# Attention with mixed heads: scores as scaled float16 parts on row halves, premix on array quarters, float32 postmix with the sums folded in

## The chip, the cores and the metric
The kernel runs on one core of a Trainium2 chip. The metric is device time in microseconds, the median of several executions. TensorE (PE) multiplies matrices and writes PSUM, VectorE (DVE), ScalarE (ACT) and GpSimd (POOL) work elementwise, and SyncE (SP) issues the transfers. An array quarter is one half of TensorE's rows with one half of its columns.

## The reference
Two batches, 12 heads, 448 tokens, head size 64; model width 768. The scores of all heads are mixed by a 12 x 12 matrix before the softmax, and the softmax's results by another after it. Then follow an RMS norm, a gated block (768 to 1536 to 768) and a second block (768 to 2048 to 768).

```python
scores = scale * np.matmul(q, k.transpose(0, 1, 3, 2))
scores = np.einsum('bhij,hg->bgij', scores, w_pre)
attn = np.exp(scores - np.max(scores, axis=-1, keepdims=True))
attn = attn / (np.sum(attn, axis=-1, keepdims=True) + 1e-09)
attn = np.einsum('bhij,hg->bgij', attn, w_post)
x = np.matmul(attn, v)                       # to [tokens, 768]
xn = x / np.sqrt(np.mean(x * x, -1) + 1e-6) * rms_g
x = (silu(xn @ w_gate) * (xn @ w_val)) @ w_out
out = elu(x @ w_in2) @ w_out2
```

## The kernel before
Operands are split in a high and a low part, x = h + l, and three products (hh, hl, lh) are summed in PSUM.

The attention has a first stage and a loop. In the first stage the q and k of the first batch are turned by TensorE to [head size, token] (`k_turn`, `q_turn`) and split. q's two parts stand one above the other on 128 partitions, and k twice, so that `scores` (L407, L408) needs two 128-row products per head and chunk of 112 query rows. ScalarE copies the scores out of PSUM as float32 (`scores_out`, L418), and a transfer puts them into the DRAM tensor `s_d`, as [query row, head, key].

The loop takes 90 groups, 45 for each batch. A group is ten query rows with all heads, 120 partitions (row, head), read back from `s_d` two groups at a time into `sg` (`load_group`). Its steps are, each for another group at the same time:
- premix (`g_premix`): a 120 x 120 matrix with `w_pre` on its diagonal blocks. Every other group takes float32 as it is (L476), the others split parts (`g_split` on ScalarE, L468, and GpSimd, L469; products L479 to L481).
- the maximum on VectorE (L488), the exponential with its sum on ScalarE (L496), the sum's reciprocal (L504, L511).
- the exponentials over their sum, as float16 parts `eh` (L524 on ScalarE or L526 on VectorE) and `el` (L533 on VectorE).
- postmix (`g_postmix`, L554): four chunks of 112 keys, three float16 products each, which also turn the result.
- `g_out` (L566): ScalarE copies the result into `at`, and after six or seven groups a window's product with v follows (L590), the norm, and the split of the normed tokens.

Between these steps a list `hq` is worked off at fixed rates per step (`FAST`, `RATE`, `LATE`): the first batch's other score chunks, then the turning of the second batch, then its scores. All engines take their instructions in the program's order. Five PSUM tiles (`psa`) serve scores, premix and turning alike. `psa` tiles are given out as they are freed in the program's order.

After the attention, weights come as float64, are converted to split parts beside the products (`convert`), with the norm's weights `g_sb` multiplied into gate and value weights, and TensorE goes through all products of the two blocks.

## Time and profile before
| | us |
|---|---|
| median of 3 runs | 789.88 (789.84 to 791.38) |
| span of the profiled execution | 787.3 |
| TensorE busy | 759.4 |
| VectorE busy | 550.6 |
| ScalarE busy | 445.6 |
| GpSimd busy | 114.4 |

The profiled execution's own time is its span, from the first to the last instruction; the runs' times include what lies around it. Busy time counts records, and the records of matmuls reach to their modelled end, so two that follow each other overlap: the price of a matmul is read from one start to the next. PEld is the loading of weights, which runs beside matmuls.

### The profile page before, as it was taken

To read this page: it belongs to the slowest core of one execution; us is meant where nothing else is said; L and a number is where in the kernel's file an instruction comes from. 1 tells how busy PE (TensorE), PEld (TensorE's weight loads), DVE (VectorE), ACT (ScalarE), POOL (GpSimd) and SP (SyncE) were. 2 spreads that over 40 slices of the span, in tenths; PEclk is the share of its full clock that TensorE was granted. 3 is DMA by queue.
4 is the path that set the end of the run, shared out by engine and by line. 5 is a ranking of instruction groups with operands and counts; after the bars stand their busy time and mean duration, and the time that the engine had idled before them with its cause. 6 is when DMAs were issued, how large, how long until landed. Compare 5 with 4: busy or idle time off the path is not lost.

```text
span 787.3 us, 14708 instructions
## 1 busy us (share of the span) xinstructions
PE 759.4 (96%) x5655; PEld 673.1 (85%) x5655; DVE 550.6 (70%) x1135; ACT 445.6 (57%) x952; POOL 114.4 (15%) x141
## 2 busy tenths in 40 slices
PE   6779999999998999999999999999999999999997
PEld 5557778777776779999999999999999999999997
DVE  6356999665789938887877865652898887553651
ACT  7679888887987925654544433231576566221320
POOL 4212565333443400000000000000000000000000
PEclk9899999999998999999999999999999999999999
DMA  7798665668783303343332333231444343433512
GB/s 205 222 280 252 168 154 140 178 173 236 217 230 78 104 2 121 122 132 108 121 112 94 116 121 106 95 121 41 121 132 120 109 122 100 111 111 111 155 47 70
DMA packets 90249, 105.42 MB, mean 134 GB/s; under 512 B 16004, under 2 KB 86084, under 8 KB 90180
## 3 DMA queue, kind: packets, MB, share of 16 engines
q1 hardware_dynamic: 90180, 104.49, 46.0%
q8 instruction: 44, 0.72, 0.4%
q14 instruction: 25, 0.20, 0.1%
HBM read 82.46 MB, written 22.02 MB: 133 GB/s over the span
## 4 chain that ended last, share of the span: by engine, by line
PE 83%; DVE 7%; DMA 5%; ACT 2%; issue 1%; SPq 1%; POOL 1%; ACTq 0%; POOLq 0%
PE psa_t L197 13%; PE psa_t L198 13%; PE psa_t L199 13%; PE psv_t L590 5%; PE pst_t L554 4%; PE psf_t L198 4%; PE psf_t L199 4%; PE psf_t L197 4%; PE psa_t L966 3%; PE psa_t L964 3%; PE psa_t L965 3%; DMA s_d<-st 3%; PE psa_t L476 3%; DMA sg<-s_d 2%; PE psa_t L407 2%; DVE el L533 1%
## 5 line engine op out<-in xcount | busy, mean ns | idle before, releaser
L554 PEld LDWEIGHTS <-eh 120*112 120x112 f16 x720 | 66.8, 131 | 27.2 <-issue 21.8
L240 ACT ACTIVATE whl<-w 128x768 fp32r<-128x768 f32 x44 | 37.1, 844 | 86.0 <-PE psf_t L966 28.5
L244 ACT ACTIVATE whl<-w,g_sb 128x128 fp32r<-128x128 f32 x144 | 45.0, 393 | 64.1 <-PE psa_t L199 25.6
L219 ACT ACTIVATE w<-raw 128x768 f32<-128x768 f32 x68 | 62.5, 919 | 30.5 <-DVE whl L251 23.6
L469 POOL TENSOR_TENSOR sl<-sg,sh 120x448 fp32r<-120x448 f32 (+1 forms) x45 | 54.5, 1211 | 116.2 <-ACT sh L468 111.6
L251 DVE TENSOR_TENSOR whl<-w,whl 128x768 fp32r<-128x768 f32 x44 | 42.2, 958 | 41.1 <-ACT whl L240 40.0
L198 PE MATMUL psa_t<-x2l,whl 128*128 128x448 f32 x192 | 70.1, 365 | 0.0
L199 PE MATMUL psa_t<-x2h,whl 128*128 128x448 f32 x192 | 70.1, 365 | 0.0
L197 PE MATMUL psa_t<-x2h,whl 128*128 128x448 f32 x192 | 70.1, 365 | 0.0
L233 DVE SCALAR_TENSOR_TENSOR w<-w,raw 128x768 int32<-128x768 int32 x68 | 65.2, 958 | 2.3
L554 PE MATMUL pst_t<-m2h,eh 120*112 120x120 f16 x360 | 63.0, 217 | 2.7 <-ACT at L566 2.6
L227 DVE SCALAR_TENSOR_TENSOR raw<-raw 128x768 int32<-128x768 int32 x68 | 64.8, 953 | 0.0
L554 PE MATMUL pst_t<-m2h,el 120*112 120x120 f16 x360 | 63.1, 218 | 1.7 <-DVE el L533 1.7
L496 ACT ACTIVATE e<-psa_t,nmax 120x448 f32<-120x448 f32 (+1 forms) x90 | 58.0, 645 | 11.4 <-DVE rs L511 10.4
L533 DVE SCALAR_TENSOR_TENSOR el<-e,rs,eh 120x448 f16<-120x448 f32 (+1 forms) x90 | 64.0, 711 | 0.3 <-ACT eh L524 0.3
L554 PE MATMUL pst_t<-m2l,eh 120*112 120x120 f16 x360 | 63.0, 218 | 0.0
L488 DVE TENSOR_REDUCE nmax<-psa_t 120x1 f32<-120x448 f32 (+1 forms) x90 | 55.2, 613 | 8.4 <-PE psa_t L481 8.3
L197 PE MATMUL psa_t<-xh,whl 128*128 128x448 f32 x150 | 55.7, 372 | 1.0 <-ACT xh L640 1.0
L590 PE MATMUL psv_t<-at,vs 112*64 112x70 f32 (+3 forms) x1344 | 55.7, 230 | 0.0
L590 PEld LDWEIGHTS psv_t<-at,vs 112*64 112x64 f32 x1344 | 46.5, 139 | 9.9 <-issue 7.0
L198 PE MATMUL psa_t<-xl,whl 128*128 128x448 f32 x150 | 54.9, 366 | 0.0
L199 PE MATMUL psa_t<-xh,whl 128*128 128x448 f32 x150 | 54.8, 365 | 0.0
(167 smaller groups left out, 2059.2 us busy)
## 6 DMA issues: line engine op xcount, KB each, us to landing
raw<-in_moe_w_out_dram SPq DMA_DIRECT2D x28, 768.0 KB, 4.5
sg<-s_d SPq DMA_DIRECT2D x44, 420.0 KB, 5.0
s_d<-st SPq DMA_DIRECT2D x93, 196.0 KB, 3.2
raw<-in_moe_w_in_dram SPq DMA_DIRECT2D x16, 768.0 KB, 4.7
raw<-in_moe_w_gate_dram SPq DMA_DIRECT2D x12, 768.0 KB, 4.3
raw<-in_moe_w_val_dram SPq DMA_DIRECT2D x12, 768.0 KB, 4.4
vs<-in_v_dram SPq DMA_DIRECT2D x4, 672.0 KB, 7.7
kt<-in_k_dram SPq DMA_DIRECT2D x12, 224.0 KB, 3.8
```

The costliest lines, as they stand in the source:

```text
L197: nc.tensor.matmul(out=ps, lhsT=wh(kk), rhs=xh_(kk), start=(first and kk == 0), stop=False)
L198: nc.tensor.matmul(out=ps, lhsT=wh(kk), rhs=xl_(kk), start=False, stop=False)
L199: nc.tensor.matmul(out=ps, lhsT=wl(kk), rhs=xh_(kk), start=False, stop=(last and kk == nk - 1))
L219: nc.scalar.activation(out=w, in_=raw.bitcast(F32)[:, :, 1], func=ACTF.Copy, scale=REBASE)
L227: nc.vector.scalar_tensor_tensor(out=lo, in0=hi, scalar=SIGN, in1=lo, op0=ALU.bitwise_and, op1=ALU.bitwise_or)
L233: nc.vector.scalar_tensor_tensor(out=wi, in0=wi, scalar=3, in1=lo, op0=ALU.logical_shift_left, op1=ALU.bitwise_or)
L469: nc.gpsimd.tensor_tensor(out=sl[:r], in0=s32, in1=sh[:r].bitcast(F32), op=ALU.subtract)
L488: nc.vector.tensor_reduce(out=nmax[:r], in_=ps[:r, :S], axis=AXX, op=ALU.max, negate=True)
L496: nc.scalar.activation(out=e32[:r], in_=ps[:r, :S], func=ACTF.Exp, bias=nmax[:r], scale=1.0, accum_out=sm[:r])
L533: nc.vector.scalar_tensor_tensor(out=el[:r], in0=e32[:r], scalar=rs[:r], in1=eh[:r], op0=ALU.mult, op1=ALU.subtract)
L554: nc.tensor.matmul(out=o, lhsT=lhs[:r, c * CP:(c + 1) * CP], rhs=rhs[:r, :, :ni], start=(n == 0), stop=(n == 2),)
L590: nc.tensor.matmul(out=psx[s * D:(s + 1) * D, kk, :n], lhsT=vs[b][:, hh, c, :], rhs=at[:, c, hh, :n], start=(c == 0), stop=(c == NCH - 1),)
```

## The change
- **Scores.** q and k of two heads are turned side by side, so that one head stands on partitions 0 to 63 and the other on 64 to 127 (`turn`). `scores` makes three products per head, each on its half of TensorE's rows, alternating between the two heads and writing a PSUM tile for each. The result is multiplied by a scale per head, `alpha`, from the largest q and k, and leaves as two float16 parts: the high one by ScalarE, the low one by VectorE. `s_d` holds both, in the same bytes.
- **Premix.** A group's ten rows are two halves of five rows (60 partitions at 0 and 64). Two groups are premixed together in float16, three products for each half, on the four quarters of the array. The split of `sg`, the whole-float32 form and their knobs are gone. The scale is taken back in the exponential (`esc`).
- **Postmix.** The exponentials stay float32. The reciprocal sums are multiplied into the postmix matrix by GpSimd (`g_scale`), and the postmix is one float32 product per chunk. `eh` and `el` are gone, and the loop has one step of lag less. Of the copies out of the postmix every other one goes to VectorE.
- **Norm weights.** They are multiplied into the tokens by GpSimd in the window's chain, no longer into the gate and value weights.
- The rates and the head start of `hq` are set anew; the first row chunk's scores come after all heads are turned, since `alpha` needs the largest values of all.

```diff
-            nc.tensor.matmul(out=ps[:CP, :S], lhsT=lhs, rhs=kh, start=True, stop=False)
-            nc.tensor.matmul(out=ps[:CP, :S], lhsT=lhs, rhs=kl, start=False, stop=True)
+            for n, (i, j) in enumerate(((0, 0), (0, 1), (1, 0))):
+                for s in range(2):
+                    d = slice(s * D, (s + 1) * D)
+                    nc.tensor.matmul(
+                        out=pss[s][:CP, :S], lhsT=qkt[d, 0, i, c * CP:(c + 1) * CP], rhs=qkt[d, 1, j],
+                        start=(n == 0), stop=(n == 2),
+                    )
+            def high(s):
+                a = alpha[b][:CP, 2 * p + s:2 * p + s + 1]
+                nc.scalar.activation(out=st[:, s, 0], in_=pss[s][:CP, :S], func=ACTF.Copy, scale=a)
+            def low(s):
+                a = alpha[b][:CP, 2 * p + s:2 * p + s + 1]
+                nc.vector.scalar_tensor_tensor(
+                    out=st[:, s, 1], in0=pss[s][:CP, :S], scalar=a, in1=st[:, s, 0], op0=ALU.mult, op1=ALU.subtract
...
-            nc.scalar.activation(out=sh[:r], in_=s32, func=ACTF.Copy)
-            nc.gpsimd.tensor_tensor(out=sl[:r], in0=s32, in1=sh[:r].bitcast(F32), op=ALU.subtract)
...
-                nc.tensor.matmul(out=ps[:r, :S], lhsT=m1f[:r, :r], rhs=sg.pop((b, g))[:r], start=True, stop=True)
-                nc.tensor.matmul(out=ps[:r, :S], lhsT=m1h[:r, :r], rhs=sh[:r], start=True, stop=False)
-                nc.tensor.matmul(out=ps[:r, :S], lhsT=m1l[:r, :r], rhs=sh[:r], start=False, stop=False)
-                nc.tensor.matmul(out=ps[:r, :S], lhsT=m1h[:r, :r], rhs=sl[:r], start=False, stop=True)
+            pss = [ps_a() for _ in range(n)]
+            for i, (m, x) in enumerate(((m1h[b], 0), (m1l[b], 0), (m1h[b], 1))):
+                for j in range(n):
+                    for s in range(2):
+                        c = s ^ j
+                        a = slice(s * Q, s * Q + min(HB, (rows_of(g + j) - c * HI) * H))
+                        nc.tensor.matmul(
+                            out=pss[j][c * Q:(c + 1) * Q, :S], lhsT=m[a], rhs=t[a, j, x],
+                            start=(i == 0), stop=(i == 2),
+                        )
...
-                nc.vector.tensor_scalar_mul(eh[:r], e32[:r], rs[:r])
-            nc.vector.scalar_tensor_tensor(
-                out=el[:r], in0=e32[:r], scalar=rs[:r], in1=eh[:r], op0=ALU.mult, op1=ALU.subtract
-            )
+            nc.gpsimd.tensor_scalar_mul(m2s[:GQ], m2f[:GQ], rs[:GQ])
...
-                for n, (lhs, rhs) in enumerate(((eh, m2h), (eh, m2l), (el, m2h))):
-                    nc.tensor.matmul(
-                        out=o, lhsT=lhs[:r, c * CP:(c + 1) * CP], rhs=rhs[:r, :, :ni],
-                        start=(n == 0), stop=(n == 2),
-                    )
+                nc.tensor.matmul(
+                    out=o, lhsT=e32[:GQ, c * CP:(c + 1) * CP], rhs=m2s[:GQ, :, :ni], start=True, stop=True
+                )
...
-        EARLY, FAST, RATE, LATE = 4, 1.5, 1.4, 1.4
+        EARLY, FAST, RATE, LATE = 2, 0.75, 1.1, 0.6
```

On TensorE, in the loop's first third, before: a head's scores, the premix of a group in split parts, and the beginning of its postmix (`eh`, `el` are the exponentials' parts, `m2h` and `m2l` the postmix matrix's).

```order
L407 MATMUL psa_t<-par 112x448
L408 MATMUL psa_t<-par 112x448
L479 MATMUL psa_t<-sh,m1h 120x448
L480 MATMUL psa_t<-sh,m1l 120x448
L481 MATMUL psa_t<-sl,m1h 120x448
L554 LDWEIGHTS eh
L554 MATMUL pst_t<-m2h,eh 112x120
L554 LDWEIGHTS eh
L554 MATMUL pst_t<-m2l,eh 112x120
L554 LDWEIGHTS el
L554 MATMUL pst_t<-m2h,el 112x120
```

On TensorE at the same place now, with buffer numbers and the semaphores that are waited for: the last two of a premix's twelve quarter products, the postmix, and the scores of two heads.

```order
L478 LDWEIGHTS m1h0_108
L478 MATMUL psa_t_890<-sg_717,m1h0_108 64x448
L533 MATMUL pst_t_909<-m2s_857,e32_820 112x120 [waits PE_49,Activation_49,Pool_49]
L533 MATMUL pst_t_909<-m2s_857,e32_820 112x120 x3
L408 MATMUL psa_t_915<-par_190 112x448 [waits DVE_49]
L408 MATMUL psa_t_916<-par_190 112x448 [waits Activation_49]
L408 MATMUL psa_t_915<-par_190 112x448
```

The postmix now waits for GpSimd's scaled matrix, the first score tile for VectorE's low part of an earlier score, and the second for ScalarE.

On VectorE, two steps while the second batch is scored, before: sum, maximum, reciprocal, low part, and in one of them the high part.

```order
L504 TENSOR_SCALAR sm<-sm 120x1
L488 TENSOR_REDUCE nmax<-psa_t 120x1
L511 RECIPROCAL rs<-sm 120x1
L533 SCALAR_TENSOR_TENSOR el<-e_2428,rs,eh 120x448
L504 TENSOR_SCALAR sm<-sm 120x1
L488 TENSOR_REDUCE nmax<-psa_t 120x1
L511 RECIPROCAL rs<-sm 120x1
L533 SCALAR_TENSOR_TENSOR el<-e_2483,rs,eh 120x448
L526 TENSOR_SCALAR eh<-e_2554,rs 120x448
```

On VectorE two such steps now, of which one has scores of two heads and a copy out of the postmix.

```order
L505 TENSOR_SCALAR sm<-sm 124x1
L488 TENSOR_REDUCE nmax<-psa_t 124x1
L489 TENSOR_SCALAR nmax<-nmax,esc_106 124x1
L509 RECIPROCAL rs<-sm 124x1
L419 SCALAR_TENSOR_TENSOR st<-psa_t,alpha_105,st 112x448 x2
L616 TENSOR_TENSOR xt<-xt,psa_t 128x420
L505 TENSOR_SCALAR sm<-sm 124x1
L488 TENSOR_REDUCE nmax<-psa_t 124x1
L489 TENSOR_SCALAR nmax<-nmax,esc_106 124x1
L509 RECIPROCAL rs<-sm 124x1
L419 SCALAR_TENSOR_TENSOR st<-psa_t,alpha_105,st 112x448 x2
L548 COPY at<-pst_t 112x48x10
```

The parts of the exponentials are gone from VectorE; low parts of the scores, a scaling of the maximum and copies of the postmix stand there instead, behind the maximum of the same step.

## Rows read from the trace of the kernel before
**Rows 1.** Stretches, the loop and the products after it: busy us of each engine (instructions).
```profile
core 0 of [0], span 787.3 us
core 0: us, PE busy (x) PEld busy (x) DVE busy (x) ACT busy (x) POOL busy (x), PEclk, DMA share, GB/s
39.40:273.10 233.70, 222.27 (x2700) 173.44 (x2699) 183.90 (x493) 197.48 (x476) 97.24 (x112) 0.99 0.69 186
293.60:700.00 406.40, 406.35 (x2032) 378.79 (x2033) 302.93 (x524) 197.21 (x383) 0.00 (x0) 1.00 0.36 111
```
**Rows 2.** Timeline of TensorE in the loop: start, duration, engine, line, operation, tiles.
```profile
134.72 1.01 PE L476 MATMUL psa_t<-sg,m1f 120*120 120x448 f32 x2
135.57 0.22 PE L554 MATMUL pst_t<-m2h,eh 120*112 120x120 f16 x1
...
136.18 0.44 PE L407 MATMUL psa_t<-par 128*112 128x448 f32 x1
136.46 0.37 PE L408 MATMUL psa_t<-par 128*112 128x448 f32 x1
136.66 0.34 PE L631 MATMUL psa_t<-dg,ones 70*128 70x70 f32 x2
136.80 0.44 PE L479 MATMUL psa_t<-sh,m1h 120*120 120x448 f32 x1
137.08 0.37 PE L480 MATMUL psa_t<-sh,m1l 120*120 120x448 f32 x1
137.28 0.36 PE L481 MATMUL psa_t<-sl,m1h 120*120 120x448 f32 x1
137.49 0.21 PE L554 MATMUL pst_t<-m2h,eh 120*112 120x120 f16 x1
...
139.06 1.15 PE L590 MATMUL psv_t<-at,vs 112*64 112x60 f32 x32
140.14 1.01 PE L476 MATMUL psa_t<-sg,m1f 120*120 120x448 f32 x2
```
**Rows 3.** Timeline earlier in the loop: turning k and q; weight loads of a premix.
```profile
102.42 0.56 PE L379 MATMUL psa_t<-ident,kt 112*128 112x112 f32 x4
...
102.75 0.51 PE L393 MATMUL psa_t<-identr,qn 112*128 112x112 f32 x4
...
107.94 0.28 PEld L476 LDWEIGHTS psa_t<-sg,m1f 120*120 120x120 f32 x2
```
**Rows 4.** VectorE by line in the loop: count, busy us, mean ns, idle before.
```profile
L533 DVE SCALAR_TENSOR_TENSOR el<-e,rs,eh 120x448 f16<-120x448 f32 (+1 forms) x88 | 62.6, 712 | 0.0
L488 DVE TENSOR_REDUCE nmax<-psa_t 120x1 f32<-120x448 f32 (+1 forms) x89 | 54.5, 613 | 0.1
L526 DVE TENSOR_SCALAR eh<-e,rs 120x448 f16<-120x448 f32 (+1 forms) x40 | 24.9, 623 | 0.0
...
L504 DVE TENSOR_SCALAR sm<-sm 120x1 f32<-120x1 f32 (+1 forms) x89 | 13.2, 149 | 53.3 <-ACT e L496 52.6
...
L386 DVE TENSOR_TENSOR par<-psa_t,par 128x448 fp32r<-128x448 f32 x7 | 4.3, 611 | 0.0
```
**Rows 5.** ScalarE by line in the loop.
```profile
L496 ACT ACTIVATE e<-psa_t,nmax 120x448 f32<-120x448 f32 (+1 forms) x89 | 57.4, 645 | 11.4 <-DVE rs L511 10.4 <-DVE nmax L488 0.9
L566 ACT ACTIVATE at<-pst_t 112x480 f32<-112x480 f32 (+1 forms) x86 | 50.5, 587 | 1.0 <-PE pst_t L554 0.9
...
L524 ACT ACTIVATE eh<-e,rs 120x448 f16<-120x448 f32 x48 | 32.7, 681 | 0.0
L468 ACT ACTIVATE sh<-sg 120x448 fp32r<-120x448 f32 (+1 forms) x43 | 25.2, 585 | 6.0 <-DMA sg<-s_d 4.9 <-POOL sq L605 0.9
L496 ACT ACTIVATION_READ_ACCUMULATOR e<-psa_t,nmax 120x1 f32 (+1 forms) x89 | 19.3, 217 | 0.0
```
**Rows 6.** GpSimd by line in the loop.
```profile
L469 POOL TENSOR_TENSOR sl<-sg,sh 120x448 fp32r<-120x448 f32 (+1 forms) x44 | 53.3, 1212 | 107.5 <-ACT sh L468 102.9 <-PE psa_t L481 4.3
...
L604 POOL TENSOR_TENSOR sq<-sq 128x210 f32<-128x210 f32 (+2 forms) x11 | 8.7, 795 | 0.9
```
**Rows 7.** Timeline, the first softmax exponential.
```profile
39.39 0.63 ACT L496 ACTIVATE e<-psa_t,nmax 120x448 f32<-120x448 f32 x1
```

More of the change, by code (lines that the diff above doesn't have):

```diff
@@ L47, in block_kernel @@
     GP = GI * H
+    HI = GI // 2
+    HB = HI * H
+    Q = P // 2
+    GQ = Q + HB
     NG = -(-S // GI)
@@ new lines, in post @@
+        def post():
+            ps = ps_a()
+            nc.tensor.matmul(
+                out=ps[:, :H], lhsT=selr.rearrange("p s r -> p (s r)"), rhs=wpo, start=True, stop=True
+            )
+            for s in range(2):
+                h = slice(s * Q, (s + 1) * Q)
+                nc.vector.tensor_tensor(
+                    out=m2f[h, :, s * HI:(s + 1) * HI], in0=mask[h].rearrange("p i g -> p g i"),
+                    in1=ps[h, :H].unsqueeze(2).to_broadcast([Q, H, HI]), op=ALU.mult,
+                )
@@ L707, in attention @@
         fast = len(hq)
-        hq += [lambda: q_split(*heads[H])]
-        hq += [f for i in range(H, 2 * H) for f in turn(i)]
+        for p in range(NP):
+            hq.append(lambda p=p: turn(1, p, 0))
+            hq.append(lambda p=p: (turn(1, p, 1), p + 2 < NP and load_qk(1, p + 2)))
+        hq += scales(1)
         turned = len(hq)
-        hq += [f for c in range(NCH) for f in rows(1, c)]
+        hq += [lambda p=p, c=c: scores(1, p, c) for c in range(NCH) for p in range(NP)]
         seq = [(b, g) for b in range(B) for g in range(NG)]
@@ L747, in fill @@
                 gates.pop(0)()
-        for t in range(-6, n + 5):
+        for t in range(-6, n + 4):
             if LG * 2 <= t + 5 < n and seq[t + 5][1] % LG == 0:
```

532 lines of the change are left out of this document (238 added, 294 removed).

## The prediction
> **What bounds it now.** I read the table of stretches first, for where TensorE has room, then its timeline in the loop for the price of each form, then the other engines' groups by line. The profiled execution spans 787.3 us [rows 1], which lies 2.6 us under the median of 789.88, which I keep as the constant around the span. From 293.6 us on, TensorE is busy 406.35 of 406.40 us up to 700 [rows 1]: the weight products are bound by TensorE and nothing of the change touches their matmuls. The merged scaling of the gate and value weights (one instruction for six on ScalarE and on VectorE) is worth nothing there; it would matter only if conversion became late, and VectorE is idle a quarter of that stretch. So the question is the attention part: 39.4 us until the first softmax, a loop of 90 groups (ten rows each) in 233.7 us, a tail of 20.5 us.
>
> In the loop TensorE is busy 222.3 us of 233.7 and so waits 11.4 us in all; ScalarE is busy 197.5 and VectorE 183.9 [rows 1]. A group takes 2.60 us: TensorE sets it, and the other two are close behind. The timeline of TensorE [rows 2] gives its prices, start to start, since matmuls overlap in their records:
> - a 448-column pass of split float32: 0.20 us (137.08 to 137.28);
> - the same after another form of instruction: 0.28 (136.18 to 136.46, 136.80 to 137.08), so a change of form costs some 0.08 to 0.10;
> - the whole-float32 premix: 0.85 (134.72 to 135.57), about 0.75 of it for 448 columns in two records, 0.10 the change;
> - the split premix: 0.69 (136.80 to 137.49);
> - a postmix of twelve float16 products of 120 columns: 0.61 (135.57 to 136.18);
> - a head's score chunk: 0.48 (136.18 to 136.66), 0.40 when another stands before it; I use 0.45;
> - the v product of one window piece, 32 records of 60 columns on two column halves: 1.08 (139.06 to 140.14). At the premix's price per column (0.75 us for 896) one after another they would take 1.6, so column halves do overlap.
>
> **The change, part by part, on TensorE.**
> Premix. Two groups cost 0.85 + 0.69 = 1.54; 45 such pairs are 69. After it, 12 products of 448 columns serve two groups, four to a pass, one in each quarter of the array. If quarters overlap: 3 x 0.20 + 0.10 = 0.70, 45 pairs 32, **-38**. If only column halves do: 1.30 a pair, -11. If nothing does: 2.50, +43. I take the first: the v product shows column halves overlapping; row halves no row shows.
> Scores. 84 heads' chunks (96 less the 12 ahead of the loop) cost 84 x 0.45 = 38. After it a pair of heads takes three passes on two row halves: 0.70 if they overlap, so 42 x 0.70 = 29, **-9**; one after the other 1.30, +17.
> Postmix. Twelve float16 products become four float32 ones of two records. By the premix's column price, 120 x 0.75/448 = 0.20 each, 0.80 for four, 0.90 with the change of form, against 0.61: 90 x 0.29 = **+26**. Without the change of form +17. The far bound is weight loads that nothing hides: 0.28 for two [rows 3], 1.12 for eight, +101. The v product is the nearer row, float32 records with few columns and a weight load each: 1,920 columns in 1.08, so 960 in 0.54, and with no halves to overlap 0.80, the matmul price itself. I keep +26.
> Turning the second batch. A head's two turns cost 0.33 for k (102.42 to 102.75 [rows 3]) and about as much for q; 12 heads 8. After it twelve turns of a pair, 4: **-4**.
> TensorE in all: -38 - 9 + 26 - 4 = **-25**, from 222 to 197 us of 90 groups, 2.19 a group.
>
> **The other engines.** VectorE loses the second parts (62.6) and first parts (24.9) of the exponentials [rows 4] and twelve casts of q (0.61 each, 7). It gains a second part for each score chunk, 84 between the 0.611 of L386 (same PSUM source) and the 0.712 of L533 (same operation); at 0.64, 54. It also gains half the copies out of the postmix, 45 of 480 columns at L386's rate, 29; 90 more single-column operations at 0.149, 13; and twelve maxima, 5. Sum +101 - 95 = +6: 190 us. ScalarE loses L468 (25.2), L524 (32.7), half of L566 (25) and the q splits: from 197 to about 110 [rows 5]. GpSimd loses 53.3 us of L469 and the q splits, and gains 90 scalings of 120 columns (0.80 for 210 columns [rows 6]; by the column 0.45, in all 41) and fourteen multiplications by the norm's weights (by the column 1.6 at most, 22). It stays near 110 us, off the path; but the scaling stands between the sum of a row and the postmix, two steps later, so a late one is waited for by TensorE directly. The transfers move the same bytes, two float16 values for a float32, the stores in half as many issues; at a share of 0.69 in the loop [rows 1] they stay hidden at 2.4 us a group too. A store now waits in SP's queue for VectorE's second part instead of ScalarE's copy, and the loads of later groups stand behind it; they are issued five steps ahead of their premix, which covers a step's delay.
>
> So TensorE stays the longest engine with 197, VectorE comes to 190, and ScalarE has room. The gain of 25 is not all kept. While the second batch is turned, a step's VectorE work is 0.61 maximum, three times 0.15, 0.33 copy, 1.1 x (0.61 + 0.40) for the turns and 0.27 for the windows, 2.77; reduced like its sum for overlapping ends by a seventh (the loop's 21 groups by line, the largest in [rows 4], sum to 218, its busy time is 183.9) 2.35, against 2.15 on TensorE: 23 steps x 0.2 = 5. And the PSUM tiles: five in all; a premix now takes two at once, the second held a step longer, and a score tile is freed by VectorE's second part, which stands behind the maximum, where before ScalarE freed it first thing in the step. TensorE's waits in the loop were 11.4; I add half again, 6. Together **+11**.
>
> Start and tail. The first batch's scores now wait until all six pairs are turned and the largest q and k are known; before, head 0 was scored while head 2 was turned. ScalarE's 24 copies and the 12 second parts (12 x 0.61 = 7.3) fill that time, while the old first step was held up anyway until 39.39 [rows 7]. I take **+2**, between 0 and +8. The loop's lag is one step shorter; the last windows have one more multiplication on GpSimd: **-1**.
>
> Sum: 787.3 - 25 + 11 + 2 - 1 = 774.3; with the 2.6 around the span, **777 us**.
>
> **A rule against it.** The row that bears on the quarters is the v product: two halves that write different partitions of one PSUM tile overlap, 1.08 against 1.6 [rows 2]. It has two column halves and one set of rows. The Trainium skill, TensorEngine Tiling (Array Packing), section Restrictions and Gotchas, says that different row tiles cannot access the same PSUM bank at the same time. The trace cannot contradict it. By it, the first two quarters of a pass, which are on different rows and write one tile, would follow one another. The same page (Tiling Modes, Key Properties) says that a change of mode drains the engine; the trace agrees with a cost, 0.08 to 0.10 us a change, which the terms have.
>
> **The rivals.**
> (a) Quarters pass in two slots instead of one, since the two row halves of a group write one tile: a pass is 0.40, a pair 1.30, the premix saves 11 instead of 38. TensorE then stands at +2, the give-back from VectorE shrinks to the 6 of the tiles, and 789.9 + 2 + 6 + 1 = **799**. It decides from a pass of 0.32 on: then the 25 less the 11 and the 1 are used up. For it: no row shows row halves side by side. Against: column halves in one tile do overlap.
> (b) Row halves never overlap, in the scores neither: -11 + 17 + 26 - 4 = +28, no give-back: **819**. The same evidence, further off.
> (c) Everything overlaps, but the step is set by a circle rather than by an engine: maximum, exponential, PSUM tile, next premix, next maximum. Over two steps by [rows 4, 5]: premix 0.70 and its latency 0.2, maximum and its scaling 0.76, second parts 1.28, a copy 0.65, single columns 0.45, windows 0.27, second maximum 0.76, exponential 0.65 + 0.22: 5.9, less a seventh of VectorE's 4.2, 5.3 or 2.65 a step where scores are made. With 60 such steps and 30 of 2.3 the loop takes 228, with the turning steps in it too 238: **785 to 795**. It decides from a mean of 2.59 on. For it: the two busiest engines would be within 4% of each other, and the release stands behind the maximum. Against: in before, with a balance nearly as close, TensorE waited 5% only.
> (d) It goes better: the postmix at +17, no VectorE-bound stage; 777 - 9 - 5 = **763**.
>
> **Chances.** Forecast 0.45 (its own range 768 to 786), (d) 0.10, (a) 0.13, (b) 0.12, (c) 0.20, of which I count 0.06 faster and 0.08 slower. Differences under 0.2% (1.6 us, about what a measurement of this kernel can tell) are no change: the middle of (c) and the fringe of the forecast, 0.07. Faster 0.60, same 0.07, slower 0.33. The range from 757 to 804 leaves out (b), the fringe of (a) and a little below (d), together 0.2.
>
> **What would show it.** Start to start on TensorE: four premix products within 0.20 to 0.25 us, a pair of heads' scores in 0.7, a postmix in 0.8 to 0.9. A loop of 220 us (first to last softmax) with TensorE near 197 busy by starts and VectorE near 190. ScalarE's busy time down by some 85 us. The stretch after the attention unchanged in length, 493 us. I am wrong if the premix's twelve products take over 1.2 us, if a postmix takes over 1.2, if VectorE's second parts take 0.8 or more (84 x 0.16 = 13 us more, on an engine without room), or if the first softmax comes after 48 us.

## The result and the profile after
The changed kernel takes 793.19 us in the median (790.23 to 801.45, 11 runs) against 789.84 (787.0 to 791.43, 11 runs): ratio 1.0059, 95% interval 1.0033 to 1.0085. It is **slower** by 0.6%, where 777 was predicted. The profiled execution took 797.66, span 795.9.

Stretches of the changed kernel: start, loop (first to last softmax), products.
```profile
core 0: us, PE busy (x) PEld busy (x) DVE busy (x) ACT busy (x) POOL busy (x), PEclk, DMA share, GB/s
0.00:48.90 48.90, 33.24 (x143) 21.40 (x143) 32.13 (x65) 27.13 (x49) 2.63 (x18) 1.00 0.60 160
48.90:281.70 232.80, 215.27 (x2723) 162.92 (x2723) 194.10 (x578) 144.43 (x321) 100.11 (x158) 0.98 0.65 183
302.20:700.00 397.80, 397.60 (x1981) 370.04 (x1982) 280.44 (x407) 173.79 (x272) 0.00 (x0) 1.00 0.36 111
```
Beside [rows 1, 7]: the first softmax comes at 48.95 instead of 39.39, **9.6 us later**; the loop takes 232.8 instead of 233.7, the stretch from it to the products 20.5 in both, the rest the same to 0.3 us. The 8.6 us of span are the start less a loop that gave back 1. ScalarE lost 53 us in the loop, VectorE gained 10, TensorE lost only 7.

TensorE's timeline in the changed loop, for the prices of [rows 2]:
```profile
86.10 0.86 PE L408 MATMUL psa_t<-par 64*112 64x448 f32 x6
86.89 0.71 PE L570 MATMUL psv_t<-at,vs 112*64 112x70 f32 x16
87.53 1.07 PE L533 MATMUL pst_t<-m2s,e 124*112 124x120 f32 x8
88.53 0.71 PE L570 MATMUL psv_t<-at,vs 112*64 112x70 f32 x16
89.17 0.38 PE L478 MATMUL psa_t<-sg,m1h 60*64 60x448 f16 x4
89.38 0.36 PE L478 MATMUL psa_t<-sg,m1l 60*64 60x448 f16 x4
89.57 0.36 PE L478 MATMUL psa_t<-sg,m1h 60*64 60x448 f16 x4
89.86 1.07 PE L533 MATMUL pst_t<-m2s,e 124*112 124x120 f32 x8
90.86 0.86 PE L408 MATMUL psa_t<-par 64*112 64x448 f32 x6
```
Start to start, twelve quarter products take 0.69 (89.17 to 89.86; each four start within 10 ns), a postmix 1.00, a pair of heads' scores 0.79.

VectorE, ScalarE and GpSimd by line in the changed loop, for [rows 4 to 6] (one view, by engine):
```profile
L488 DVE TENSOR_REDUCE nmax<-psa_t 124x1 f32<-124x448 f32 x89 | 54.7, 615 | 1.7 <-PE psa_t L478 1.7
L419 DVE SCALAR_TENSOR_TENSOR st<-psa_t,alpha,st 112x448 f16<-112x448 f32 x74 | 46.9, 677 | 14.3 <-ACT st L415 13.6
L548 DVE COPY at<-pst_t 112x480 f32<-112x480 f32 (+1 forms) x44 | 28.2, 641 | 0.0
...
L498 ACT ACTIVATE e<-psa_t,nmax,esc 124x448 f32<-124x448 f32 x90 | 65.4, 727 | 35.4 <-DVE rs L509 31.4 <-DVE nmax L489 2.4 <-DVE ms L597 1.6
...
L516 POOL TENSOR_SCALAR m2s<-m2f,rs 124x120 f32<-124x120 f32 x88 | 61.5, 699 | 155.9 <-DVE rs L509 134.8 <-DVE dg L609 5.7 <-PE psa_t L383 5.4
...
L533 PE MATMUL pst_t<-m2s,e 124*112 124x120 f32 (+1 forms) x696 | 95.8, 283 | 6.4 <-POOL m2s L516 4.9 <-DVE sm L505 1.4
L478 PE MATMUL psa_t<-sg,m1h 60*64 60x448 f16 x352 | 39.4, 381 | 7.8 <-DMA sg<-s_d 4.4 <-DVE st L419 3.1
```
The start of the changed kernel, timeline of several engines in order of time (SPq is the issue of transfers):
```profile
24.50 9.61 SPq L423 DMA_DIRECT2D s_d<-st  x6
...
37.22 0.80 SPq L450 DMA_DIRECT2D sg<-s_d  x2
38.07 0.85 SPq L423 DMA_DIRECT2D s_d<-st  x2
38.97 1.45 SPq L450 DMA_DIRECT2D sg<-s_d  x2
40.37 0.55 PE L478 MATMUL psa_t<-sg,m1h 60*64 60x448 f16 x1 [0.39 <-DMA sg<-s_d]
40.46 7.09 SPq L423 DMA_DIRECT2D s_d<-st  x3
43.74 1.16 ACT L415 ACTIVATE st<-psa_t,alpha 112x448 f16<-112x448 f32 x2 [5.47 <-DMA s_d<-st]
45.15 0.58 PE L478 MATMUL psa_t<-sg,m1h 60*64 60x448 f16 x2 [3.54 <-DVE st L419]
48.95 0.73 ACT L498 ACTIVATE e<-psa_t,nmax,esc 124x448 f32<-124x448 f32 x1
```
The first premix starts at 40.37 and gets its second PSUM tile at 45.15. That tile was held by scores whose ScalarE copy waited 5.47 us for a score buffer, whose store stood in SP's queue behind the first group load. Ahead of it VectorE, busy 19.6 us of the old start, is busy 32.1 of the new: six maxima of q and k at 1.21, 23 second parts of scores at 0.68.

### The profile page after: what moved, and what is told of

Its sections match the earlier page's. It is cut to its first block, busy times and chain, and to the rows that moved or that the text cites. A ratio compares the mean times of both kernels' runs of the same rounds, so it can differ in the third digit from the quotient of the medians.

```text
span 795.9 us, 14330 instructions
## 1 busy us (share of the span) xinstructions
PE 757.1 (95%) x5626; PEld 662.1 (83%) x5626; DVE 555.5 (70%) x1123; ACT 369.1 (46%) x673; POOL 108.7 (14%) x184
## 4 chain that ended last, share of the span: by engine, by line
PE 80%; DVE 9%; DMA 5%; ACT 2%; issue 2%; POOL 1%; SPq 1%; ACTq 0%; DVEq 0%; POOLq 0%
PE psa_t L106 13%; PE psa_t L107 12%; PE psa_t L108 12%; PE pst_t L533 7%; PE psv_t L570 4%; PE psf_t L108 4%; PE psf_t L106 4%; PE psf_t L107 4%; PE psa_t L930 3%; PE psa_t L929 3%; PE psa_t L928 3%; PE psa_t L478 3%; PE psa_t L408 3%; DMA sg<-s_d 3%; DVE st L419 2%
## 5 line engine op out<-in xcount | busy, mean ns | idle before, releaser
L152 DVE TENSOR_TENSOR whl<-w,whl 128x768 fp32r<-128x768 f32 x68 | 65.1, 958 | 65.9 <-ACT whl L148 64.8
L533 PEld LDWEIGHTS pst_t<-m2s,e 124*112 124x112 f32 x720 | 82.6, 182 | 28.9 <-issue 13.9
L533 PE MATMUL pst_t<-m2s,e 124*112 124x120 f32 x720 | 98.7, 283 | 6.4 <-POOL m2s L516 4.9
L516 POOL TENSOR_SCALAR m2s<-m2f,rs 124x120 f32<-124x120 f32 x90 | 63.5, 706 | 157.1 <-DVE rs L509 135.4
L498 ACT ACTIVATE e<-psa_t,nmax,esc 124x448 f32<-124x448 f32 x90 | 65.4, 727 | 35.4 <-DVE rs L509 31.4
L415 ACT ACTIVATE st<-psa_t,alpha 112x448 f16<-112x448 f32 x96 | 55.5, 632 | 47.7 <-PE psa_t L408 14.4
L419 DVE SCALAR_TENSOR_TENSOR st<-psa_t,alpha,st 112x448 f16<-112x448 f32 x96 | 61.0, 678 | 23.6 <-ACT st L415 22.9
L488 DVE TENSOR_REDUCE nmax<-psa_t 124x1 f32<-124x448 f32 x90 | 55.3, 615 | 1.7 <-PE psa_t L478 1.7
L408 PE MATMUL psa_t<-par 64*112 64x448 f32 x288 | 52.2, 458 | 3.7 <-DVE st L419 3.3
L929 PE MATMUL psa_t<-whl,gh 128*128 128x384 f32 x160 | 53.5, 334 | 0.0
```

The lines of the kernel that those rows point to most:

```text
L152: nc.vector.tensor_tensor(out=whl[:, 1], in0=st["w"], in1=whl[:, 0].bitcast(F32), op=ALU.subtract)
L408: nc.tensor.matmul(out=pss[s][:CP, :S], lhsT=qkt[d, 0, i, c * CP:(c + 1) * CP], rhs=qkt[d, 1, j], start=(n == 0), stop=(n == 2),)
L419: nc.vector.scalar_tensor_tensor(out=st[:, s, 1], in0=pss[s][:CP, :S], scalar=a, in1=st[:, s, 0], op0=ALU.mult, op1=ALU.subtract)
L498: nc.scalar.activation(out=e32[:GQ], in_=ps[:GQ, :S], func=ACTF.Exp, bias=nmax[:GQ], scale=esc[b][:GQ], accum_out=sm[:GQ])
L533: nc.tensor.matmul(out=o, lhsT=e32[:GQ, c * CP:(c + 1) * CP], rhs=m2s[:GQ, :, :ni], start=True, stop=True)
L929: nc.tensor.matmul(out=o, lhsT=gh[:, kk, tk], rhs=wl[:, j], start=False, stop=False)
```

## The experiments
The table gives for each run (4 to 10 executions) the median and the ratio to the kernel before, and from its profile the first softmax and the loop, in us. Each ratio is one of means, against executions of the kernel before made beside that run (their medians lie between 788.89 and 790.37).

| run | first softmax | loop | median | ratio (95%) |
|---|---|---|---|---|
| before | 39.39 | 233.7 | 789.84 | 1 |
| changed | 48.95 | 232.8 | 793.19 | 1.0059 (1.0033 to 1.0085) |
| e1 | 45.05 | 266.4 | 824.9 | 1.0447 (1.0425 to 1.0469) |
| e2 | 46.80 | 227.6 | 792.23 | 1.0050 (1.0023 to 1.0077) |
| e3 | 48.62 | 266.1 | 833.39 | 1.0535 (1.0469 to 1.0602) |
| e4 | 48.84 | 226.7 | 791.78 | 1.0039 (1.0004 to 1.0073) |
| e5 | 45.33 | 233.3 | 797.69 | 1.0102 (1.0035 to 1.0169) |
| e6 | 49.26 | 239.8 | 805.51 | 1.0216 (1.0172 to 1.0260) |
| e7 | 48.67 | 229.8 | 793.70 | 1.0074 (1.0038 to 1.0111) |
| e8 | 44.28 | 233.6 | 794.38 | 1.0076 (1.0042 to 1.0110) |
| e9 | 47.30 | 225.9 | 792.33 | 1.0026 (0.9997 to 1.0055) |
| e10 | 45.13 | 225.4 | 788.10 | 0.9949 (0.9918 to 0.9981) |
| e11 | 38.70 | 253.5 | 810.75 | 1.0246 (1.0155 to 1.0337) |
| e12 | 48.08 | 228.3 | 792.51 | 1.0028 (0.9994 to 1.0062) |
| e13 | 50.39 | 227.8 | 795.42 | 1.0083 (1.0066 to 1.0100) |
| e14 | 49.08 | 228.5 | 792.85 | 1.0047 (1.0031 to 1.0064) |
| e15 | 44.58 | 225.4 | 788.17 | 1.0015 (0.9980 to 1.0050) |
| e16 | 48.47 | 225.2 | 794.10 | 1.0065 (1.0047 to 1.0083) |
| e17 | 43.79 | 225.3 | 785.84 | 0.9976 (0.9952 to 1.0000) |
| e18 | 47.01 | 229.4 | 792.73 | 1.0041 (1.0022 to 1.0060) |

Runs that left the loop's order alone (e2, e9, e10, e12 to e17) show it at 225 to 228.5. The changed kernel's profiled loop is 4 to 8 us above that. In it two loads came late, the later of which is seen in its chain of work (start, us, what), with the granted clock behind it (the third number from the right) in a stretch of 3.4 us:
```profile
236.69 11.24 DMA sg<-s_d
247.94 0.04 issue
247.98 1.33 PE psa_t L478 x11
249.31 1.89 PE pst_t L533 x8
```
```profile
248.00:251.40 3.40, 3.40 (x22) 2.56 (x22) 0.93 (x4) 0.18 (x1) 2.67 (x5) 0.50 0.30 92
```
The load took 11.2 us from issue to landing, TensorE waited, its granted clock fell to 0.50, and its next postmix took 1.89 instead of 1.00. So the usual execution should be start +9.6 and loop -5 to -8, which fits the median's +3.4; this is argued from the other runs, since the changed kernel has one profile.

### What sets the loop
**e3** made the postmix one pass:
```diff
-            e32 = ap.tile([P, S], F32, tag="e32", name="e32", bufs=5)
+            e32 = ap.tile([P, S], F32R, tag="e32", name="e32", bufs=5)
...
-            m2s = ap.tile([P, H, GI], F32, tag="m2s", name="m2s", bufs=3)
+            m2s = ap.tile([P, H, GI], F32R, tag="m2s", name="m2s", bufs=3)
```


> The postmix's two factors are written as float32r, so that each product is one pass with rounded factors instead of whole float32 (fewer bits than the reference asks; nothing else is changed). TensorE then loses about half of the 0.98 us that a postmix occupies, 90 x 0.45 = 40 us of the loop's 215. Theory T (TensorE's own work still sets the step, its products are only dearer than predicted: 215 busy of 233): the loop falls from 232.8 to about 205 (VectorE's 194 is next), time down by 20 to 30 us, to 763 to 773. Theory C (the circle maximum, exponential, PSUM tile, next premix sets the step; the postmix is not in it): loop at least 226, time down by 7 us at most. Theory V (VectorE's 194 us with its waits set it): the same as C, down by 10 at most.


It was slower by 40 us, outside every theory. Its timeline of TensorE, and its stretches:
```profile
88.15 0.58 PE L478 MATMUL psa_t<-sg,m1l 60*64 60x448 f16 x4
88.53 0.58 PE L478 MATMUL psa_t<-sg,m1h 60*64 60x448 f16 x4
89.04 1.00 PE L533 MATMUL pst_t<-m2s,e 124*112 124x120 f32 x4
89.97 1.46 PE L408 MATMUL psa_t<-par 64*112 64x448 f32 x6
...
110.89 0.58 PE L533 MATMUL pst_t<-m2s,e 124*112 124x120 f32 x4
111.30 0.57 PE L383 MATMUL psa_t<-ident,qk 112*128 112x112 f32 x4
```
```profile
110.00:120.00 10.00, 8.16 (x109) 5.91 (x107) 9.86 (x30) 5.86 (x13) 3.05 (x5) 1.00 0.69 156
120.00:130.00 10.00, 8.43 (x96) 7.03 (x98) 8.46 (x25) 5.64 (x15) 4.55 (x9) 0.66 0.75 194
140.00:150.00 10.00, 10.00 (x105) 7.62 (x104) 6.09 (x24) 3.75 (x10) 4.43 (x6) 0.50 0.27 72
```
The postmix did become cheap, 0.41 at 110.89 against 1.00. But TensorE worked at its lower level through most of the loop: at 88 the passes start 0.38 apart and the postmix takes 0.93, and after a stretch with 8.2 of 10 us busy the granted clock falls to 0.66 and then to 0.50 (1.2 GHz of 2.4); in 16 of the 20 stretches of 10 us from 120 to 320 it is at most 0.73. Until 107 us it had stood at that level from the start, fully busy from 70 on; why it rose so late stays open. With less work on TensorE its work was slower, and the loop longer by 33 us. On the three theories the run decides nothing.

**e4** made VectorE's second parts cheap:
```diff
-                nc.vector.scalar_tensor_tensor(
-                    out=st[:, s, 1], in0=pss[s][:CP, :S], scalar=a, in1=st[:, s, 0], op0=ALU.mult, op1=ALU.subtract
+                nc.vector.tensor_copy(out=st[:, s, 1], in_=st[:, s, 0])
+                nc.vector.tensor_scalar(
+                    out=junk[:, s], in0=pss[s][:CP, :8], scalar1=a, scalar2=None, op0=ALU.mult
```


> VectorE's second part of each score chunk (0.677 us, float32 from PSUM) is replaced by a copy of the float16 first part from SBUF to SBUF and an 8-column operation on the PSUM tile, so that the order and the release of the tile stay; the second part stored is not the reference's. An estimate of 0.35 us for the two takes 0.33 x 84 = 28 us from VectorE's 194 in the loop. Theory T (TensorE sets the step): loop down by 5 us at most. Theory C (circle): two second parts stand in the circle of two steps where scores are made, 0.65 us less in 42 such pairs of steps, loop down by 12 to 25. Theory V (VectorE sets it): loop down by 20 to 28. The start gains 1 to 3 us in each.


Stretch of the loop:
```profile
48.80:275.60 226.80, 213.89 (x2723) 162.62 (x2723) 179.03 (x651) 144.63 (x321) 101.83 (x158) 0.97 0.66 188
```
VectorE loses 15 us (194 to 179, where 28 were expected: the copies were dearer than estimated), and the loop is that of e2 and e9 to 1 us. Theories V and C do not show, even scaled to 15 us; T holds.

**e6** premixed in halves:
```diff
-                        in_=x[:, 1:3] if s else x[:, 0:4:3],
+                        in_=x[:, s:4:2],
...
-                        c = s ^ j
+                        c = s
```


> Both groups of a premix pair use the two quarters on the diagonal (rows s to columns s) and not all four, with their rows loaded to match; the twelve products then pass two at a time in six passes instead of four at a time in three. TensorE gets 3 x 0.20 us more for each of 45 pairs, 27 us. Theory T (TensorE's products set the step): loop up by 20 to 27 us, time 813 to 820. Theory V (VectorE or another engine sets it and TensorE has some 15 us of room): loop up by 12 us at most, time under 805. If four quarters did not really pass side by side: no change.


Stretch of the loop:
```profile
49.20:289.10 239.90, 231.43 (x2723) 172.12 (x2723) 195.00 (x578) 143.88 (x321) 100.01 (x158) 0.99 0.62 177
```
Against e9 (211.2 busy in 225.9) TensorE has 20 us more (27 were expected) and the loop 14; the time is 12 above the changed kernel's. That lies between the theories, nearer to V: most of TensorE's work is on the path, some third of an addition falls into its waits. And four quarters do pass side by side: on the diagonal each four products take 0.38 to 0.41 (132.59, 133.00, 133.38), in the changed kernel 0.20.

**e7** moved the row sum behind the maximum:
```diff
-            at_step(g_sum, t - 1)
             at_step(g_max, t)
+            at_step(g_sum, t - 1)
```


> VectorE adds the constant to the row sums of group t-1 after the maximum of group t instead of ahead of it; nothing else. The sum waits for the exponential of t-1, so in the changed kernel exponential, sum, maximum, its scaling and the next exponential form a chain of 0.73 + 0.15 + 0.61 + 0.21 and latencies, which is the shortest step seen there, 1.82 to 1.89 us (before: 1.52 to 1.62). Theory T (TensorE sets the mean step of 2.6): the short steps shrink, the long ones grow, loop within 3 us. Rival (this chain with the waits it hands on sets the pace): loop down by 8 to 20 us.


Short steps fell from 1.82 to as little as 0.69, long ones grew, the loop stayed (229.8, with two steps of 5.6). The chain is not what sets the mean step; theory T holds.

**e11** put the float32 postmix alone into the kernel before:
```diff
-                for n, (lhs, rhs) in enumerate(((eh, m2h), (eh, m2l), (el, m2h))):
...
+                nc.tensor.matmul(
+                    out=o, lhsT=e32[:r, c * CP:(c + 1) * CP], rhs=m2s[:r, :, :ni], start=True, stop=True
+                )
...
-                at_step(g_high, t - 1)
+            at_step(g_scale, t - 1)
-            at_step(g_postmix, t - 3)
+            at_step(g_postmix, t - 2)
```


> The kernel before with one part of the change alone: float32 postmix on the exponentials as they are, the row sums put into the matrix by GpSimd; premix, scores, turns and start stay. VectorE loses 87 us of parts, ScalarE 33; TensorE's postmix goes from 0.64 to the 0.98 that it took in the changed kernel, 90 x 0.34 = 30 us. Theory T (TensorE sets the step, and the postmix eats what the premix gives): loop 233.7 to 258 to 265, time 814 to 822. Theory V (the other engines set it): loop 220 to 232, time 776 to 788. My prediction's price for the part (+26) gives 816.


Stretch of the loop, TensorE's largest wait (us, times, longest), and a postmix in its timeline:
```profile
38.70:292.20 253.50, 235.61 (x2371) 189.83 (x2372) 112.69 (x366) 173.96 (x430) 141.10 (x204) 0.99 0.62 172
```
```profile
PE pst_t L528 <- POOL m2s L510: 16.8, 13, 2.9
```
```profile
133.43 0.98 PE L528 MATMUL pst_t<-m2s,e 120*112 120x120 f32 x8
134.17 0.52 PE L385 MATMUL psa_t<-identr,qn 112*128 112x112 f32 x4
```
VectorE falls by 71 us and the loop grows by 19.8, so theory V falls and TensorE sets the loop, but by less than the 24 to 31 that T expected. TensorE's work grew by 13 us and not by 30: here a postmix takes 0.74 (133.43 to 134.17), not the 1.00 of the changed kernel. The rest is waiting, 16.8 us in all for GpSimd's scaled matrix, which stands behind the splits there.

### What sets the start
**e1** and **e5** made fewer scores ahead of the first premix, e5 with the rate made up later:
```diff
-        EARLY, FAST, RATE, LATE = 2, 0.75, 1.1, 0.6
+        EARLY, FAST, RATE, LATE = 0, 0.75, 1.1, 0.6
...
-            if t > -6:
+            if t > -2:
```
```diff
-                done += FAST if popped < fast else RATE if popped < turned + NP else LATE
+                done += (FAST if t < 1 else 0.9) if popped < fast else RATE if popped < turned + NP else LATE
```


> No score chunk of the second row is made ahead of the first premix (EARLY 0, and the counter of pieces starts at step -1 instead of -5). In the changed kernel the first premix's second PSUM tile came at 45.2 us, held by score chunks whose ScalarE copy waited 5.47 us for a store that stood in SP's queue behind the load of the first group. Theory S1 (that circle of queue, score buffer and PSUM tile costs the start 5 to 6 us): first premix ends near 41, first softmax near 43 instead of 48.95, time down by 5 to 6 us, to about 787.5, if the five pieces find room in the loop later. Rival S2 (the start is set by loads, maxima and the landing of the first stores, and the pieces only fill a wait): first softmax still 47 to 49, time within 2 us of 793.

> As e1, but the loop's score schedule is kept: EARLY is 0, the counter of pieces still starts at step -5 (three pieces before the first premix instead of five, so that each finds a free score buffer), and from step 1 on it runs at 0.9 instead of 0.75 until the two pieces are made up. Theory S1 (five pieces need more buffers than there are, and the fourth and fifth hold PSUM tiles until a store lands): first softmax 43 to 45.5 instead of 48.95, loop as in the changed kernel (227 to 233), time 4 to 6 us under its 793.2, that is 787 to 789. Rival (moving the pieces costs in the loop what it gives at the start, as the 17 us steps of e1 could also mean): time 792 or more.


Both got the start (3.9 and 3.6 us), so the circle of S1 is there. Neither kept it. In e1 the list `hq` fell behind and a whole row of scores was forced ahead of a load (36 products in one step): single steps of 17.05 us, twice. In e5 the loop is 233.3, against 225 to 228.5 where the order was left alone; the rival holds. The list's head start is worth as much as the tiles it blocks.

**e2** took a constant scale and scored between the turns; **e9** issued the first loads from another queue; **e10** both:
```diff
-            nc.vector.tensor_reduce(
-                out=mq[0][:, :, 2 * p:2 * p + 2], in_=x.rearrange("p t h c d -> p t h (c d)"), axis=AXX, op=ALU.max,
+        nc.vector.memset(mq[0], 5.0)
...
+            if i > 1:
+                scores(0, i - 2, 0)
...
```
```diff
-        def load_group(b, g0):
+        def load_group(b, g0, eng=nc.sync):
...
-        load_group(0, 0)
+        load_group(0, 0, nc.gpsimd)
...
-        load_group(0, LG)
+        load_group(0, LG, nc.gpsimd)
```


> The maxima of q and k of the first batch are left out (a constant 5.0 stands in their place, so the scale is not taken from the data) and the scores of pair i-2 are made beside the turns of pair i, as the kernel before did. Theory S2 (waiting for the largest values before the first score costs the start): six maxima of 1.21 us leave VectorE and the six pairs of scores lie beside the turns; the last store lands at 26 to 29 us instead of 37, first softmax 38 to 41, time down by 8 to 10 us, to 783 to 785. Theory S1 alone (the circle of SP's queue, score buffer and PSUM tile): the stores land earlier, but the 5.5 us behind the first load stay. If S1 is all there is, less than 3 us is gained.

> The changed kernel with the first two group loads issued from GpSimd's queue instead of SP's; no piece of the loop is moved. The stores of the two early pairs then need not stand behind a load that waits for the last store of the first row. Theory S1 (queue, score buffer and PSUM tile hold the first premix's second tile): first softmax 44 to 46 instead of 48.95 (e5 with fewer pieces gave 45.3), and, since the loop's order is the old one, loop as in e2 (227 to 230); time 787 to 789. Rival (the transfers themselves share the DMA engines and the start is set by their sum): first softmax 47.5 to 49, time 791 to 794.

> e2 and e9 together: no maxima of the first batch (a constant in their place), first scores beside the turns, first loads from GpSimd's queue. Theory: the 9.5 us of the start are the sum of the wait for the maxima and the circle behind the first load; then each alone leaves the other in place, and both together bring the first softmax to 38 to 41, time to 781 to 785. Rival (a third cause, such as the 1.21 us maxima apart, TensorE at its lower clock, or the DMA engines): first softmax 43 or later.


The first softmax came 2.2, 1.7 and 3.8 us earlier. They add up, but to less than half of 9.6; the 44 to 46 expected of e9 and the 38 to 41 expected of both were misses. In e9 the premix got both tiles at once, but at 42.99: its load, issued at 37.47, now shared the transfers with the stores that had been held back.

**e8** and **e12** gave the first row six score buffers, on e5 and on e9:
```diff
+            if b == 0 and c == 0 and p < 3:
+                if p == 0:
+                    big_st[0] = ap.tile([CP, NCH * H * WMAX], F32, tag="at", name="st0", bufs=2).bitcast(F16)
+                st = big_st[0][:, p * 4 * S:(p + 1) * 4 * S].rearrange("p (s t j) -> p s t j", s=2, t=2)
```


> e5, and the first three pairs' scores take their float16 parts in a piece of the buffer of the first window, so that the six pairs of the first row have six buffers instead of three. In the changed kernel ScalarE waited for a store's landing ahead of four of those pairs (0.52, 1.05, 0.59, 0.36 us). Theory S1: first softmax 1.5 to 3 us ahead of e5's. Rival (the stores share the DMA engines and the last one lands no earlier): less than 1 us.

> e9 and the six buffers for the first row's scores (as in e8), with the loop's order untouched: the version that should be fastest if theory S1 holds. First softmax 42.5 to 44.5, loop 227 to 230, time 785 to 788, below the kernel before. Rival as for e9: first softmax 46 or later, time 790 or more.


e8's start is 1 us better than e5's, e12's 0.8 worse than e9's. e12 gains no time over e9 (792.51 against 792.33), and e8's 794.38 against e5's 797.69 is within the spread of their few executions: the buffers are not it, and e12 is not the faster version expected.

**e13** gave TensorE filler products; **e14**, **e15** and **e16** added them to e9, e10 and e12:
```diff
+        def warm(k):
+            for _ in range(k):
+                nc.tensor.matmul(out=wt[:, :P], lhsT=ident, rhs=ones, start=True, stop=True)
...
+        warm(20)
         side_by_side(0)
...
             turn(0, i, 1)
+            warm(2)
...
```


> The changed kernel with products of two constants, whose result nobody reads, put on TensorE where it is idle in the start: 20 ahead of the first turn, 2 behind each pair's turns, 4 behind each step of the scales, 6 ahead of the first premix. In the kernel before TensorE's passes of 448 columns fall from 0.37 to 0.20 us start to start at 11.7 us; in the changed kernel they stay at 0.37 until 46 us (a pair's scores 1.46, its turns 1.76). Theory H (TensorE is kept at half speed through the start, and that is the third cause): with the fillers passes of 0.20 before 20 us, a pair's scores 0.7 to 0.8, first softmax 43 to 46.5 instead of 48.95, time 787 to 791. Rival (VectorE's maxima and the queue set the start, TensorE's speed is hidden): first softmax within 1 us of 48.95, time 792 or more.

> e13 and e9 together: fillers, and the first two group loads from GpSimd's queue. Theory H with S1: first softmax 41 to 44, loop 225 to 229, time 783 to 787, faster than before by 0.3 to 0.9 per cent. Rival: as e9, 790 to 793.

> e10 (constant scale, first scores beside the turns, own queue) with the fillers. In e10 TensorE was the engine that was waited for in the start: turns 1.76 and scores 1.46 us a pair, 3.2 each. Theory H: at full speed 1.65 a pair, six pairs 9 us less, of which the other engines give half; first softmax 38 to 42 (before: 39.4), time 781 to 785. Rival (loads and stores set it): first softmax 44 or later, time 787 or more.

> e14 with the six score buffers of e12, which by itself gained nothing. With TensorE at full speed the score buffers may be what is waited for: by theory H and S1 1 to 2 us under e14, 782 to 786. Rival: no difference from e14 beyond 1 us.


In the changed kernel the turns of two pairs take 3.66 us (sixteen transposes from 13.78 on). With the fillers, timelines of TensorE and ScalarE:
```profile
14.32 1.12 PE L389 MATMUL psa_t<-ident,qk 112*128 112x112 f32 x8 [0.32 <-ACT qk L368]
15.28 0.62 PE L221 MATMUL warm_t<-ones,ident 128*128 128x128 f32 x4
...
23.63 1.46 PE L414 MATMUL psa_t<-par 64*112 64x448 f32 x12
...
50.39 0.73 ACT L504 ACTIVATE e<-psa_t,nmax,esc 124x448 f32<-124x448 f32 x1
```
A pair is turned in 0.96, and two pairs' first scores take 1.46 together instead of 1.46 each: TensorE had reached its faster level, which it lost again behind them (the granted clock is 0.50 from 29.8 to 40.1). The Trainium skill, TensorE: Matmul & The Clock Gate, Part 1, says that the clock gate lets pass more or fewer pulses by how busy the engine has lately been; the trace agrees in direction (0.96 a pair turned behind the fillers, 1.83 without). But the first softmax came 1.4 us later, not earlier, so theory H is not borne out; nor is it settled. The fillers themselves put the first scores 2.6 us later (23.63 against 21.04), of which the first row had made up 1.1 when its last second part was done (35.24 against 33.78), and from 29.8 on the scores ran at the lower level again. e14 and e16 came no earlier than e9 and e12, and e15, where no maxima are waited for, is 0.6 us ahead of e10; their expected starts were missed.

**e17** moved e10's premix constants to between the turns, **e18** moved e9's score piece behind the first exponential:
```diff
+                (None, None, sc[4], sc[5], sc[6], post)[i]()
                 scores(0, i - 2, 0)
```
```diff
+                done += (FAST + {-1: -FAST, 1: FAST / 2, 2: FAST / 2}.get(t, 0)) if popped < fast else RATE if popped < turned + NP else LATE
```


> e10 (constant scale, scores beside the turns, own queue for the first loads), with the small steps that make the premix constants moved from behind the fourth pair's scores to between the turns. In e10 and e15 the fifth pair's scores waited 1.9 to 2.1 us for them and the sixth pair's copies stood 3.5 us behind; that place was mine, not the changed kernel's. If the start is a chain of VectorE's and ScalarE's steps a pair (turn, scores) with nothing else in it: the last store lands some 3 us earlier than in e10, first softmax 41 to 43 instead of 45.13, time 784.5 to 787. Then 48.95 less 42 is the price of taking the scale from the data plus the queue. Rival (the first row's stores and the first loads set it, 8 us from the last score to the first premix, as in the kernel before): first softmax 44 or later.

> e9 with the score piece of step -1 moved behind the first exponential (made up in steps 1 and 2), scale from the data as in the changed kernel. In e9 the first maximum was ready at 45.7 and the first exponential ran at 47.30, behind two copies of that piece. If that place is worth what it shows: first softmax 45.5 to 46.2, time 790 to 791.5, still no faster than before. Rival: the piece is missed later, as in e5, and the time is that of e9 (792.3) or more.


e17's first softmax is at 43.79, 1.3 earlier than e10's and between the 41 to 43 expected and the rival's 44; its time is 785.84, as expected. Its first loads, timeline of GpSimd's queue:
```profile
34.02 2.80 POOL L446 DMA_DIRECT2D sg<-s_d  x4 [30.40 <-DMA s_d<-st]
```
They are issued at 34.02 against 37.22 in the changed kernel and 28.51 in the one before. The run shows what the change is worth with a start 5.2 us shorter, a ratio of 0.998 (0.995 to 1.000), but it is no version to keep, since its scale does not come from the data. e18 gained 0.3 at the start (1.1 to 1.8 were expected) and nothing in time. No version with the scale from the data beat the kernel before.

## Why the prediction was wrong
**The first step that failed is "Start and tail"**: "I take +2, between 0 and +8". It was 9.6, past the bound of 48 us that was named as showing it wrong. The second parts of the scores were thought to fit under the old wait, and the six maxima of q and k (1.21 each) stood in no term of the start. They are a chain. Timelines of the kernel before (ScalarE's copy of the first row's last score, issue of the first group load) and of the changed one (the first row's last second parts):
```profile
25.40 0.55 ACT L418 ACTIVATE st<-pst_s 112x448 f32<-112x448 f32 x1 [0.30 <-PE pst_s L408]
28.51 0.34 SPq L440 DMA_DIRECT2D sg<-s_d  x1
```
```profile
32.50 1.28 DVE L419 SCALAR_TENSOR_TENSOR st<-psa_t,alpha,st 112x448 f16<-112x448 f32 x2 [0.94 <-ACT st L415]
```
VectorE turns and takes maxima without a break from 7.5 to 19.6, the first scores leave at 22.5, and the last second part of the first row is done at 33.8, where the kernel before, which scored between its turns, had copied its last one out at 25.95. That is 7.8 of the 9.6; the last store, which the first load waits for, lands 0.9 later behind it than it did then (load issued at 37.22), and the road from the load to the softmax is 0.9 longer. Two causes are shown by edits: waiting for the largest values, with the order that it forces (2.2 in e2, 2.2 in e10 and 3.5 in e17 against e9), and the circle of queue, score buffer and PSUM tile (1.7 in e9, 3.6 to 3.9 when the pieces are left out). Together 5.2. The other 4.4 stay open. In e17 the row leaves VectorE at 29.5, 3.6 behind the kernel before, the last store's landing takes 1.9 more, and the road to the softmax 1.1 less; that the first is the second parts on VectorE and the next the larger stores is argued from these times, not shown. TensorE's lower level stays a rival for a part of it: the changed kernel runs at it until 56.9 us, the kernel before left it at about 11 (and had it again from 31.6 to 38.4), and e13 did not settle it. Score buffers (e12) moved nothing.

**The second, and the larger, is TensorE's sum**, -25. Counting each matmul from its start to the next start, or to its own end where the engine then waits, the loop's forms give before and after: premix 68.6 to 37.4 (-31, predicted -38), scores 35.4 to 32.1 (-3, predicted -9), postmix 57.9 to 88.5 (+31, predicted +26), turns 10.3 to 6.0 (-4, as predicted); in all 222.0 to 215.4, **-7**. The premix's price was right (0.69 against 0.70), but 37.4 over 44 pairs is 0.85. About half of the missing 7 us are stalls inside a pair, where the second group's products wait for their tile or rows; the other half lies in five pairs at TensorE's lower level: two ahead of 56.9 at 1.26, two behind the late loads at 1.6, one at 107.6. The other forms paid there as well, a postmix 1.87 (53.79 to 55.66). By such rows an estimate of what the lower level cost premix, postmix and scores is 8 us in the changed loop, which spent some 18 us at it, where the loop before spent 6.8 (243.2 to 250.0).

The postmix was mis-sized by a tenth of a microsecond, 1.00 against 0.90: its eight records start 0.10 apart, as the sum had it, but a change is paid at both ends, with 0.19 behind the first record and 0.20 behind the last. e11 shows whose price that is. There the same float32 postmix stands between products on the whole array, takes 0.74 and costs 70.8 us in the loop, +13; in the changed kernel it takes 0.91 where the turning follows, which uses the whole array too, and 1.00 where scores on row halves or the v product on column halves do. So some 15 to 18 of the 31 us (about 3 of them are perhaps the lower level's) come with the new neighbours on parts of the array and not with float32; the changes of 0.08 to 0.10 that the prediction read from [rows 2] are changes of data type on the whole array. The scores pay a change too, 0.79 against 0.70.

**The give-back of 11 held**: TensorE's waits went from 11.4 to 17.5, and with the 7 by which the premix's sum is over its price that is 13. The size is in part luck, since it came from other places than thought. VectorE does not set the loop (e4), nor does the chain of exponential and maximum (e7); the waits are for group loads (4.4), GpSimd's scaled matrix (4.9; it takes 0.70 instead of the 0.45 taken by the column) and second parts that hold PSUM tiles (4.6 for premix and scores). "They stay hidden" was wrong for the transfers: two loads of 9.7 and 11.2 us show through in the profiled execution.

With the measured sizes the prediction's own sum gives 787.3 - 14 + 13 + 9.6 = 795.9, the span (-14 is the -7 with the premix at its price). That is 21.6 over the 774.3 of the prediction: 11 from TensorE's sum, of which scores and postmix have about half each, 7.6 from the start, 2 from the give-back and 1 from the tail, whose -1 did not come (20.5 us in both). Rival (a) and (b) fell: quarters whose row halves write one PSUM tile start together and twice as many pass as in e6, so the rule of the Trainium skill in TensorEngine Tiling (Array Packing), Restrictions and Gotchas, that different row tiles cannot use one PSUM bank at once, did not make itself felt in the time (0.69 for twelve). Rival (c) named the range, 785 to 795, but not the mechanism. That TensorE sets most of the loop was right (e4, e6, e7, e11).

## What to carry to other kernels
- A change that needs a value over all data before the first step is paid for in the start, where little covers it (2.2 to 3.5 of 9.6 us here); cost the start as a chain of one row, engine by engine, and not as work that fits under an old wait.
- When TensorE alternates short forms on different parts of the array, price each form with the change on both sides: here a postmix took 1.00 that took 0.74 between products on the whole array.
- Moving pieces out of a crowded start gains there and loses later, if they were the loop's head start: measure both stretches.

## What the runs showed of the hardware
- Relieving TensorE can cost time: with a postmix of 0.41 instead of 1.00 (e3) the granted clock was low through most of the loop (at most 0.73 in 16 of 20 stretches), and the kernel 40 us slower.
- TensorE's passes can start 0.37 apart, as at a granted clock of 0.50, where the profile prints 1.00: so in the changed kernel until 56.9 us, and in e3 until 107.1. The trace's records of the clock begin only there, with the rise (in the kernel before at 11.1), so ahead of it the passes tell the level and not the 1.00.
- The same float32 postmix takes 0.74, 0.91 or 1.00 us by what stands beside it on TensorE (e11 and the changed kernel), while most of its eight records start 0.10 apart in all three.
- The weight products, the same instructions in every run, go through in one of two rhythms, which lasts for the whole stretch. Stretch of 100 us in the changed kernel, and in e2:
```profile
400.00:500.00 100.00, 100.00 (x496) 92.66 (x495) 65.48 (x94) 34.13 (x51) 0.00 (x0) 1.00 0.33 105
```
```profile
400.00:500.00 100.00, 100.00 (x486) 90.81 (x485) 63.25 (x90) 34.82 (x51) 0.00 (x0) 1.00 0.34 111
```
  486 matmuls against 496 at the same granted clock: 206.7 ns a pass instead of 202.7, some 9 us of a run. e2, e5 and e9 were profiled in it; what chooses it stays open.
